# Batch 0, then the weights as fp32, in one SyncE queue, with GpSimd casting from staging buffers; both queries first

## The chip, the cores and the metric

The kernel runs on one core of a Trainium2 chip. The metric is the device time of that core in microseconds; the median of three runs before the change is 317.52 us. The profile is one execution of the same program, recorded by the hardware profiler; its times count from the start of its span. TensorE (PE) multiplies matrices, its weight loads are listed apart as PEld; VectorE (DVE) and ScalarE (ACT) work on tiles, GpSimd (POOL) can cast and issue transfers, and SyncE (SP) only issues transfers.

## What is computed

A linear attention, followed by a gated feed-forward block. Cut to what matters:

```python
q, k, v: (8 batches, 8 heads, 576 positions, 64) float32
q_s = softmax(q, over the 64)             # each row on its own
k_s = softmax(k, over the 576 positions)
kv  = einsum('bhsd,bhse->bhde', k_s, v)   # 64 x 64 for each head
x   = einsum('bhsd,bhde->bhse', q_s, kv)  # then heads side by side: (4608 tokens, 512)

g   = x @ w_gate                          # 512 -> 1536
val = x @ w_val                           # 512 -> 1536
out = (g * sigmoid(g) * val) @ w_out      # 1536 -> 512, float32
```

The kernel leaves out the subtraction of the maximum, which changes nothing in a softmax of small inputs, and multiplies in bf16 with fp32 sums.

## The kernel before

Tokens are handled batch by batch. A batch has 576 tokens and its 8 heads are two groups G of 4 heads; one tile of q, k or v of a group is 128 partitions by 2 by 576 fp32, in rows of 2304 bytes (576 KB in all). The attention of a batch writes its 512 features, transposed, to `xt`, four blocks of 128 feature rows; features are what the feed-forward sums over.

The feed-forward of a token range works in 12 units m of 128 hidden features (`m_unit`, line 286): four matmuls g_ps of `wg`, four u_ps of `wv`, each into PSUM banks, then Silu on ScalarE (`sg`, line 305) and a product on VectorE (`hr`, line 306). For the first 576 tokens every unit has two column parts, 320 and 256. `o_mm` (line 318) then multiplies `hr` with `wo`, 12 matmuls for 128 tokens, and the result is copied out and stored from the SyncE queue.

Everything on each engine is in the order in which the code is written (a manual schedule); the tile pools add the waits for buffers. Pool `ld` has three buffers for each of the tags q, k and v. What stands at the beginning, in order:

- SyncE loads q and k of batch 0, group 0 then group 1 (lines 355 to 357, `load`, line 77).
- GpSimd's queue loads v of batch 0 straight into bf16 tiles `v16`, since that queue can cast on the way (lines 358 to 361); the first of these waits for the first k. Behind them in the same queue come all weights, cast on the way as well: four slices each of `wg` and `wv`, of 256, 384, 384 and 512 columns, taken in turns, then four of `wo` (lines 380 to 383). GpSimd's time goes to issuing them.
- ScalarE takes exponentials of q and k (line 124) in pieces; VectorE sums (line 138) and scales them (line 152); TensorE turns the query (`turn_pe`, line 166), and forms key sums (line 397), kv (`kv_first`, line 411) and x (`x_mm`, line 220). `spin` matmuls on a zero tile fill TensorE's waits.
- SyncE's next loads, batches 1 and 2 (lines 454 and 455), wait for the second wo slice (`w_dma[-3]`).
- The 12 units m of batch 0 follow (line 457), and then attention of batch 1 between four o units (lines 460 to 493), in which ScalarE works in the order: first query, first key, second query, two copies of o results, second key; TensorE turns the first query, forms kv, does an o unit, and turns the second query. `cast_v` (line 127) casts v of later batches on GpSimd.
- Then seven chunks of tokens follow, each with 12 units m, four o units and the attention of a later batch in between.

Of the kernel before, what the change touches and what calls it, by code (L numbers as in the profile page):

```python
# [15 lines left out]
def kernel(  # L16
# [10 lines left out]
    nc = tc.nc  # L27
# [37 lines left out]
    def head_ap(src, b, G, t0=0, t1=T):  # L65
        return bass.AP(
            tensor=src.tensor,
            offset=src[b, 4 * G].offset + 64 * t0,
            ap=[[T * 64, 128], [2 * HSTR, 2], [1, (t1 - t0) * 64]],
        )  # L70

    def load(what, src, b, G, pieces=((0, T),), after=None):
        t_ = ld.tile([128, 2, T * 64], FP32, tag=what, name=what)
        raw[what, b, G] = t_
        last = None
        for t0, t1 in pieces:
            last = nc.sync.dma_start(out=t_[:, :, 64 * t0:64 * t1], in_=head_ap(src, b, G, t0, t1))
            if after is not None:
                tc.add_manual_dep(last.ins, after.ins.name, SYNC, reason="order of loads")
                after = None  # L80
        return last
# [10 lines left out]

    def w_slice(dst, src, c0, n):
        ap = bass.AP(
            tensor=src.tensor,
            offset=src[0, c0].offset,
            ap=[[d_ff, 128], [128 * d_ff, KT], [1, n]],
        )
        return nc.gpsimd.dma_start(out=dst[:, :, c0:c0 + n], in_=ap)

    def wo_slice(m0, n):
        ap = bass.AP(
            tensor=moe_w_out.tensor,
            offset=moe_w_out[m0 * 128, 0].offset,
            ap=[[d_model, 128], [128 * d_model, n], [1, d_model]],
        )
        return nc.gpsimd.dma_start(out=wo[:, m0:m0 + n, :], in_=ap)
# [11 lines left out]
    def exp_of(what, b, G, pieces=((0, T),)):  # L119
        s = st.setdefault((b, G), {})  # L120
        e = s["e" + what] = at.tile([128, T, 2, 64], BF16, tag="e" + what, name="e" + what)
        src = raw[what, b, G].rearrange("p h (t d) -> p t h d", d=64)
        for t0, t1 in pieces:
            nc.scalar.activation(out=e[:, t0:t1], in_=src[:, t0:t1], func=AF.Exp)  # L124
# [7 lines left out]
    def norm_sum(b, G, pieces=((0, T),)):  # L132
        s = st[b, G]
        eq2 = s["eq"].rearrange("p t h d -> p (t h) d")
        rs = at.tile([128, 2 * T], FP32, tag="rs", name="rs")
        first = None
        for t0, t1 in pieces:
            i = nc.vector.reduce_sum(  # L138
                out=rs[:, 2 * t0:2 * t1], in_=eq2[:, 2 * t0:2 * t1, :], axis=mybir.AxisListType.X
            )  # L140
            first = first or i
        rr = s["rr"] = at.tile([128, 2 * T], FP32, tag="rr", name="rr")
        nc.vector.reciprocal(out=rr, in_=rs)
        return first

    def norm_mul(b, G, pieces=((0, T),), engs=None):
        s = st[b, G]
        eq2 = s["eq"].rearrange("p t h d -> p (t h) d")
        qs = s["qs"] = at.tile([128, T, 128], BF16, tag="qs", name="qs")
        for (t0, t1), eng in zip(pieces, engs or (nc.vector, nc.vector)):  # L150
            n = 2 * (t1 - t0)
            eng.tensor_mul(  # L152
                qs[:, t0:t1, :].rearrange("p t (h d) -> p (t h) d", d=64),
                eq2[:, 2 * t0:2 * t1, :],
                s["rr"][:, 2 * t0:2 * t1].to_broadcast([128, n, 64]),
            )
# [129 lines left out]
    def m_unit(c0, n, m, by_part=False):  # L286
# [7 lines left out]
        if by_part:  # L294
            steps.sort(key=lambda a: (a[2], a[0], a[1]))
# [57 lines left out]
    with tc.manual_schedule():  # L353
        kd = []
        for G in range(NG):
            load("q", q, 0, G)
            kd.append(load("k", k, 0, G))
        d = nc.gpsimd.dma_start(out=v16[0], in_=head_ap(v, 0, 0))  # L358
        tc.add_manual_dep(d.ins, kd[0].ins.name, SYNC, reason="order of loads")
        for t0, t1 in BANKS:  # L360
            nc.gpsimd.dma_start(out=v16[1][:, :, 64 * t0:64 * t1], in_=head_ap(v, 0, 1, t0, t1))  # L361
# [11 lines left out]
        exp_of("q", 0, 0, BANKS)  # L373
        exp_of("k", 0, 0)
        exp_of("q", 0, 1, BANKS)
        first = norm_sum(0, 0, BANKS)
        norm_mul(0, 0, BANKS)
        norm_sum(0, 1, BANKS)

        for c0, n in ((0, 256), (256, 384), (640, 384), (1024, 512)):  # L380
            w_slice(wg, moe_w_gate, c0, n)
            w_slice(wv, moe_w_val, c0, n)
        w_dma = [wo_slice(m0, 3) for m0 in (0, 3, 6, 9)]
# [20 lines left out]
        def kv_first(G, t0=0, t1=T):  # L404
            s = st[0, G]
            if t0 == 0:
                s["kv"] = [bank("kv") for _ in range(2)]
            for t in range(t0, t1):
                for g in range(2):
                    r = slice(64 * g, 64 * g + 64)  # L410
                    nc.tensor.matmul(
                        out=s["kv"][g][:, 0:128].rearrange("p (h d) -> p h d", d=64),
                        lhsT=ek_of(0, G, g, t), rhs=v16[G][r, :, 64 * t:64 * t + 64],
                        start=(t == 0), stop=(t == T - 1),
                    )

        def scale_first(G, eng1):
            s = st[0, G]
            kn = s["kn"] = at.tile([128, 2, 128], BF16, tag="kn1", name="kn1")
            nc.scalar.mul(kn[:, 0, :], s["kv"][0][:, 0:128], s["kvr"][:, 0:1])  # L420
            if eng1 is nc.scalar:
                nc.scalar.mul(kn[:, 1, :], s["kv"][1][:, 0:128], s["kvr"][:, 1:2])
            else:
                nc.vector.tensor_scalar_mul(kn[:, 1, :], s["kv"][1][:, 0:128], s["kvr"][:, 1:2])

        spin(8)
        spin(6, first)
        key_sum(0)
        turn_pe(0, 0, 0)
        turn_pe(0, 0, 1)  # L430
        turn_out(0, 0, 0, nc.scalar)
        exp_of("k", 0, 1)
        turn_out(0, 0, 1, nc.scalar)
        norm_mul(0, 1, BANKS)
        spin(6)
        key_sum(1)
        kv_first(0)
        scale_first(0, nc.scalar)
        turn_pe(0, 1, 0)
        turn_pe(0, 1, 1)  # L440
        turn_out(0, 1, 0, nc.vector)
        turn_out(0, 1, 1, nc.vector)
        xp0 = x_mm(0, 0, 0), x_mm(0, 0, 1)
        kv_first(1, *BANKS[0])
        kv_first(1, *BANKS[1])
        x_out(0, 0, 0, xp0[0], (nc.scalar, nc.scalar))
        x_out(0, 0, 1, xp0[1], (nc.vector, None))
        scale_first(1, nc.vector)
        xp1 = x_mm(0, 1, 0), x_mm(0, 1, 1)
        x_out(0, 1, 0, xp1[0], (nc.scalar, nc.vector))  # L450
        x_out(0, 0, 1, xp0[1], (None, nc.vector))
        x_out(0, 1, 1, xp1[1], (nc.scalar, nc.vector))

        load_batch(1, w_dma[-3], by_group=True)
        load_batch(2)

        for m in range(MT):
            m_unit(0, S, m, by_part=(m == 0))
# [124 lines left out]
```

The softmax here doesn't subtract the row's maximum and nothing guards it: scores larger than these inputs give would overflow.

## Time and profile before

| what | value |
|---|---|
| median of three runs | 317.52 us (317.51 to 317.7) |
| the profiled run: time, span | 317.75 us, 316.0 us |
| granted TensorE clock in it | 0.998 of full speed |
| g_ps and u_ps matmuls (line 298) | 110.0 and 109.8 us busy |
| o_ps matmuls (line 322) | 93.0 us busy |
| a GpSimd cast of v, 128x1152 (line 127) | 1146 ns |
| HBM read, written | 37.75 MB, 9.44 MB |

How to read it: busy time is summed over the span, and matmuls overlap one another and their weight loads, so the shares add to more than the span. The page cuts the span into 40 slices of 7.9 us and gives the busy tenths of each engine in each. A timeline row is start, duration, engine, line, operation, output from input, and in brackets how long the engine had been idle and what ended that. A chain row is start, duration and what the end of the run can be followed back to. A window row is the stretch, its length, the busy time of PE, PEld, DVE, ACT and POOL with their instructions, then TensorE's clock, the share of the 16 DMA engines in use (over 1 where packets overlap) and GB/s. For a queue that casts, the bytes are those written.

### The profile page before, as it was taken

Reading aid. Unit: us, or ns where it says so; the run is one execution under the profiler, and the core shown is the slowest. Engines: PE = TensorE matmul, PEld = TensorE weight load, DVE = VectorE, ACT = ScalarE, POOL = GpSimd, SP = SyncE. Lnnn points to the kernel's source line nnn. Section 1 sums busy time; section 2 is a strip of 40 time slices with the busy share of each in tenths; the row PEclk is TensorE's granted clock in tenths of the full one; section 3 lists DMA queues with packets and bytes.
Section 4 is the critical chain, followed back from the end, with each engine's and each line's share of the span. In section 5 each row is a group of like instructions: output and inputs, shape, how many; then the busy total and the mean of one; then the engine's idle time right before and its main releaser. Section 6 shows DMA issues by size and latency. Waiting matters only on the chain.

```text
span 316.0 us, 4856 instructions
## 1 busy us (share of the span) xinstructions
PE 304.7 (96%) x1865; PEld 152.0 (48%) x1894; DVE 163.2 (52%) x277; ACT 147.6 (47%) x218; POOL 28.0 (9%) x35
## 2 busy tenths in 40 slices
PE   6799999999999999999999999999999999999994
PEld 2477744554444444544454444544454444444443
DVE  3834476685754566455835492639354333423421
ACT  4743488634663465447354637355743113312300
POOL 2930021100200020002000200020000000000000
PEclk9999999999999999999999999999999999999999
DMA  7999999269246806490629253944310202020124
GB/s 269 183 204 207 296 393 391 68 160 364 50 91 179 338 17 128 112 394 11 141 68 352 97 110 66 322 162 103 66 41 0 65 3 66 0 68 3 31 68 102
DMA packets 39304, 45.75 MB, mean 145 GB/s; under 512 B 16368, under 2 KB 23024, under 8 KB 39280
## 3 DMA queue, kind: packets, MB, share of 16 engines
q1 hardware_dynamic: 32480, 39.99, 42.0%
q0 software_dynamic: 6640, 5.31, 10.9%
q8 instruction: 15, 0.25, 0.3%
q10 hardware_dynamic: 160, 0.13, 0.2%
q14 instruction: 9, 0.07, 0.1%
HBM read 37.75 MB, written 9.44 MB: 149 GB/s over the span
## 4 chain that ended last, share of the span: by engine, by line
PE 88%; DMA 4%; DVE 3%; ACT 2%; issue 1%; POOL 1%; SPq 0%; DVEq 0%
PE g_ps L298 29%; PE u_ps L298 29%; PE o_ps L322 25%; PE kv L191 3%; DMA wv<-in_moe_w_val_dram 2%; DMA k<-in_k_dram 2%; DVE rs L138 1%; PE xp L267 1%; DVE qs L152 1%; PE o_ps L342 1%; ACT L124 1%; ACT eq L124 1%; POOL v L361 0%; PE tp L166 0%; POOL v L358 0%
## 5 line engine op out<-in xcount | busy, mean ns | idle before, releaser
L305 ACT ACTIVATE sg<-g_ps 128x512 bf16<-128x512 f32 (+2 forms) x120 | 65.1, 554 | 139.1 <-PE g_ps L298 120.7
L306 DVE TENSOR_TENSOR hr<-sg,u_ps 128x512 bf16<-128x512 bf16 (+2 forms) x120 | 74.5, 630 | 87.8 <-PE u_ps L298 80.4
L298 PE MATMUL g_ps<-xt,wg 128*128 128x512 bf16 (+2 forms) x469 | 110.0, 358 | 1.0 <-ACT xt L111 0.2
L298 PE MATMUL u_ps<-xt,wv 128*128 128x512 bf16 (+2 forms) x468 | 109.8, 357 | 1.2 <-DMA wv<-in_moe_w_val_dram 0.5
L322 PE MATMUL o_ps<-wo,hr 128*128 128x512 bf16 x414 | 93.0, 379 | 0.4 <-issue 0.2
L298 PEld LDWEIGHTS <-wv 128*128 128x128 bf16 x480 | 46.9, 98 | 47.2 <-DMA wv<-in_moe_w_val_dram 0.9
L298 PEld LDWEIGHTS <-wg 128*128 128x128 bf16 x480 | 45.8, 98 | 45.3 <-issue 0.7
L322 PEld LDWEIGHTS <-hr 128*128 128x128 bf16 x420 | 40.9, 98 | 49.1
L113 DVE COPY o_sb<-o_ps 128x512 f32<-128x512 f32 x33 | 22.4, 680 | 39.2 <-PE o_ps L322 37.3
L127 POOL CAST vb<-v 128x1152 bf16<-128x1152 f32 x14 | 16.0, 1146 | 174.3 <-DMA v<-in_v_dram 111.8
L138 DVE TENSOR_REDUCE rs<-eq 128x18 f32<-128x1152 bf16 (+2 forms) x18 | 21.7, 1214 | 13.2 <-ACT eq L124 13.2
L152 DVE TENSOR_TENSOR qs<-eq,rr 128x1152 bf16<-128x1152 bf16 (+2 forms) x18 | 22.1, 1237 | 0.1
L124 ACT ACTIVATE eq<-q 128x1152 bf16<-128x1152 f32 (+2 forms) x18 | 18.1, 1050 | 4.5 <-DMA q<-in_q_dram 4.4
L124 ACT ACTIVATE ek<-k 128x1152 bf16<-128x1152 f32 x16 | 18.0, 1158 | 0.3 <-DMA k<-in_k_dram 0.2
L305 ACT ACT_TABLE_LOAD x12 | 15.4, 1283 | 0.2
L124 ACT ACT_TABLE_LOAD x11 | 14.1, 1283 | 0.2
L388 PE MATMUL idle<-zero 128*128 128x512 bf16 x20 | 6.1, 459 | 3.0 <-DVE rs L138 1.8
L191 PE MATMUL kv<-vb,ek 64*128 64x129 bf16 x252 | 8.7, 217 | 0.0
L191 PEld LDWEIGHTS <-ek 64*128 64x128 bf16 x252 | 7.3, 94 | 2.7 <-ACT sg L305 2.1
L275 ACT CAST xt<-xp 128x512 bf16<-128x512 f32 x12 | 6.4, 588 | 3.6 <-PE xp L267 3.6
L276 DVE CAST xt<-xp 128x512 bf16<-128x512 f32 x12 | 7.7, 683 | 0.0
L347 ACT COPY o_sb<-o_ps 128x128 f32<-128x128 f32 x2 | 0.5, 265 | 13.3 <-DVE o_sb L346 13.3
(46 smaller groups left out, 70.2 us busy)
## 6 DMA issues: line engine op xcount, KB each, us to landing
q<-in_q_dram SPq DMA_DIRECT2D x16, 576.0 KB, 5.6
k<-in_k_dram SPq DMA_DIRECT2D x16, 576.0 KB, 7.3
out_dram<-o_sb SPq DMA_DIRECT2D x70, 128.0 KB, 2.3
v<-in_v_dram SPq DMA_DIRECT2D x14, 576.0 KB, 9.0
wo<-in_moe_w_out_dram POOLq DMA_DIRECT2D x4, 384.0 KB, 16.3
wg<-in_moe_w_gate_dram POOLq DMA_DIRECT2D x2, 384.0 KB, 9.7
wv<-in_moe_w_val_dram POOLq DMA_DIRECT2D x2, 384.0 KB, 10.7
wg<-in_moe_w_gate_dram POOLq DMA_DIRECT2D x1, 512.0 KB, 13.7
```

The costliest lines, as they stand in the source:

```text
L113: eng.tensor_copy(out=out, in_=in_)
L124: nc.scalar.activation(out=e[:, t0:t1], in_=src[:, t0:t1], func=AF.Exp)
L127: nc.gpsimd.tensor_copy(out=vbs[G][:, :, 0:128].rearrange("p t (h d) -> p t h d", d=64), in_=raw["v", b, G].rearrange("p h (t d) -> p t h ...
L138: i = nc.vector.reduce_sum(out=rs[:, 2 * t0:2 * t1], in_=eq2[:, 2 * t0:2 * t1, :], axis=mybir.AxisListType.X)
L152: eng.tensor_mul(qs[:, t0:t1, :].rearrange("p t (h d) -> p (t h) d", d=64), eq2[:, 2 * t0:2 * t1, :], s["rr"][:, 2 * t0:2 * t1].to_broadca ...
L191: nc.tensor.matmul(out=kv[g][:, c:c + 129], lhsT=ek_of(b, G, g, t), rhs=vbs[G][r, t, 0:129], start=(t == 0), stop=(t == T - 1),)
L275: nc.scalar.copy(out=xt[:, 2 * G, c0:c0 + 512], in_=main[G][0])
L276: nc.vector.tensor_copy(out=xt[:, 2 * G + 1, c0:c0 + 512], in_=main[G][1])
L298: nc.tensor.matmul(out=gu[a][i][:, 0:w_], lhsT=(wg, wv)[a][:, kk, ms], rhs=xt[:, kk, c:c + w_], start=(kk == 0), stop=(kk == KT - 1),)
L305: nc.scalar.activation(out=sg[:, 0:w_], in_=g_ps[:, 0:w_], func=AF.Silu)
L306: nc.vector.tensor_mul(hr[:, m, r:r + w_], sg[:, 0:w_], u_ps[:, 0:w_])
L322: nc.tensor.matmul(out=o_ps, lhsT=hr[:, m, r0:r0 + 128], rhs=wo[:, m, :], start=(m == 0), stop=(m == MT - 1),)
```

## The change

1. GpSimd issues no transfers. The queue of SyncE carries, in this order: both queries of batch 0, the first key, the first v, the second key, the second v; then all weights as fp32; then batches 1 and 2. The queries, the second key and the second v are each loaded as two halves of one row of heads (`by_head`), and the exponentials and sums of these are taken in the same halves.
2. The weights land in the buffers of the pool `ld`, tags q, k and v in turn (`w_load`), 20 transfers: `wg` and `wv` in slices of 128, 128 and then 256 columns, `wo` in six slices of two. GpSimd casts each to bf16 (`staged`), after v of batch 0.
3. The last half of v is cast by VectorE (384 columns) and ScalarE (192) (`cast_last`).
4. The order at the beginning is another one: both turns of queries before kv of group 0, the second kv in halves by head, other counts of `spin`, other engines for some copies.
5. Batch 1's loads no longer name a weight transfer to wait for; and `by_part`, which did the first unit m part by part, is gone.

```diff
-        t_ = ld.tile([128, 2, T * 64], FP32, tag=what, name=what)
-        for t0, t1 in pieces:
-            last = nc.sync.dma_start(out=t_[:, :, 64 * t0:64 * t1], in_=head_ap(src, b, G, t0, t1))
+        for h in ((0, 1), (1, 2)) if by_head else ((0, 2),):
+            last = nc.sync.dma_start(out=t_[:, h[0]:h[1], :], in_=head_ap(src, b, G, h))
...
+    staged = []
+
+    def w_load(dst, ap):
+        tag = ("q", "k", "v")[len(staged) % 3]
+        t_ = ld.tile([128, 2, T * 64], FP32, tag=tag, name="w" + tag)
+        n0, n1 = dst.shape[1:]
+        view = t_.rearrange("p h c -> p (h c)")[:, 0:n0 * n1].rearrange("p (a b) -> p a b", b=n1)
+        staged.append((dst, view))
+        nc.sync.dma_start(out=view, in_=ap)
...
-        for G in range(NG):
-            load("q", q, 0, G)
-            kd.append(load("k", k, 0, G))
-        d = nc.gpsimd.dma_start(out=v16[0], in_=head_ap(v, 0, 0))
-        tc.add_manual_dep(d.ins, kd[0].ins.name, SYNC, reason="order of loads")
-        for t0, t1 in BANKS:
-            nc.gpsimd.dma_start(out=v16[1][:, :, 64 * t0:64 * t1], in_=head_ap(v, 0, 1, t0, t1))
+        load("q", q, 0, 0, by_head=True)
+        load("q", q, 0, 1, by_head=True)
+        load("k", k, 0, 0)
+        load("v", v, 0, 0)
+        load("k", k, 0, 1, by_head=True)
+        load("v", v, 0, 1, by_head=True)
+        for c0, n in [(0, 128), (128, 128)] + [(c, 256) for c in range(256, d_ff, 256)]:
+            w_slice(wg, moe_w_gate, c0, n)
+            w_slice(wv, moe_w_val, c0, n)
+        for m0 in range(0, MT, 2):
+            wo_slice(m0, 2)
...
-        for c0, n in ((0, 256), (256, 384), (640, 384), (1024, 512)):
-            w_slice(wg, moe_w_gate, c0, n)
-            w_slice(wv, moe_w_val, c0, n)
-        w_dma = [wo_slice(m0, 3) for m0 in (0, 3, 6, 9)]
+        nc.gpsimd.tensor_copy(out=v16[0], in_=raw["v", 0, 0])
+        nc.gpsimd.tensor_copy(out=v16[1][:, 0, :], in_=raw["v", 0, 1][:, 0, :])
+        for dst, src in staged:
+            nc.gpsimd.tensor_copy(out=dst, in_=src)
...
+        def cast_last():
+            n = 64 * 6
+            nc.vector.tensor_copy(out=v16[1][:, 1, 0:n], in_=raw["v", 0, 1][:, 1, 0:n])
+            nc.scalar.copy(out=v16[1][:, 1, n:], in_=raw["v", 0, 1][:, 1, n:])
...
+        spin(12)
+        spin(4, first)
+        turn_pe(0, 0, 0)
+        turn_out(0, 0, 0, nc.scalar)
+        turn_pe(0, 0, 1)
+        turn_out(0, 0, 1, nc.scalar)
+        spin(7)
+        exp_of("k", 0, 0)
+        norm_mul(0, 1, BANKS)
+        key_sum(0)
+        turn_pe(0, 1, 0)
+        exp_of("k", 0, 1, True)
+        turn_out(0, 1, 0, nc.vector)
+        turn_pe(0, 1, 1)
+        turn_out(0, 1, 1, nc.vector)
+        kv_first(0)
+        scale_first(0)
+        key_sum(1)
+        cast_last()
+        xp0 = x_mm(0, 0, 0), x_mm(0, 0, 1)
+        kv_first(1, 0, 1)
+        x_out(0, 0, 0, xp0[0])
+        kv_first(1, 1, 2)
+        scale_first(1)
+        x_out(0, 0, 1, xp0[1])
+        x_one(0, 1)
 
-        load_batch(1, w_dma[-3], by_group=True)
+        load_batch(1, by_group=True)
         load_batch(2)
```

## The prediction

> **What bounds the kernel now.** I read the page's first three parts, then the chain of waits for the first 20 us, then ScalarE's and VectorE's order of work at 36 to 50 us, then windows. The page's totals:
>
> ```profile
> span 316.0 us, 4856 instructions
> PE 304.7 (96%) x1865; PEld 152.0 (48%) x1894; DVE 163.2 (52%) x277; ACT 147.6 (47%) x218; POOL 28.0 (9%) x35
> DMA  7999999269246806490629253944310202020124
> GB/s 269 183 204 207 296 393 391 68 160 364 50 91 179 338 17 128 112 394 11 141 68 352 97 110 66 322 162 103 66 41 0 65 3 66 0 68 3 31 68 102
> q1 hardware_dynamic: 32480, 39.99, 42.0%
> q0 software_dynamic: 6640, 5.31, 10.9%
> ```
>
> TensorE is busy 96% of the span, so only its idle time, some 11 us, can be won or added to; 4.6 of it lie in the first 15 us (the windows of that stretch sum to 10.4 us busy). A slice is 7.9 us: in the first seven (55 us) the DMA row reads 7, then 9s. The transfers of batches 0 to 2 and of all weights are one unbroken backlog. The GB/s row sags in slices 1 to 3 because the casting queue q0 is counted in written bf16: its 5.31 MB are 10.62 MB of fp32 read, 200 to 207 GB/s are some 410 read.
>
> The chain shows when steady work starts:
>
> ```profile
> 9.38 6.77 DMA wv<-in_moe_w_val_dram
> 16.15 0.05 issue
> 16.20 0.72 PE u_ps L298 x4
> 16.92 0.44 PE g_ps L298 x4
> ```
>
> The first wv slice ends the wait, at 16.20. Four matmuls of g_ps (0.44 us) had been done before, so TensorE runs as if from 15.76 and is then all but gapless to 44.5. The next place where an arrival matters is batch 1 (ScalarE first, then VectorE, then weight loads):
>
> ```profile
> 39.03 1.28 ACT L124 ACT_TABLE_LOAD   x1
> 40.32 1.16 ACT L124 ACTIVATE eq<-q 128x1152 bf16<-128x1152 f32 x1
> 41.39 1.15 ACT L124 ACTIVATE ek<-k 128x1152 bf16<-128x1152 f32 x1
> 43.63 1.16 ACT L124 ACTIVATE eq<-q 128x1152 bf16<-128x1152 f32 x1 [1.09 <-DMA q<-in_q_dram]
> ...
> 44.83 1.35 DVE L138 TENSOR_REDUCE rs<-eq 128x18 f32<-128x1152 bf16 x1 [0.26 <-ACT eq L124]
> ...
> 47.27 1.76 DVE L152 TENSOR_TENSOR qs<-eq,rr 128x1152 bf16<-128x1152 bf16 x1
> ...
> 44.62 0.50 PEld L166 LDWEIGHTS <-qs 128*128 128x128 bf16 x9 [0.58 <-DVE qs L152]
> 49.08 0.51 PEld L166 LDWEIGHTS <-qs 128*128 128x128 bf16 x9 [0.38 <-DVE qs L152]
> ```
>
> The exponential of batch 1's second query starts at 43.63, when its load lands (idle 1.09 us before it). From there VectorE works without a pause (reduce, reciprocal, two scales, product) until 49.03, and the second turn starts at 49.08, just as TensorE runs out (its xp matmuls before it end at 48.99). So this load has no slack: a microsecond later there is a microsecond on the end. The first query has some: the table load, not the DMA, sets 40.32.
>
> [...] from 8 to 55 us the DMA row is full whichever queue runs, so going over to one queue frees no bandwidth. [...] the product at 47.27, beside a GpSimd cast (46.67 to 47.82), took 1.76 us, the one at 43.21 alone 1.36.
>
> **The change part by part.**
>
> *SyncE's row cost.* Two windows:
>
> ```profile
> 25.00:30.00 5.00, 5.00 (x43) 3.99 (x41) 2.09 (x6) 1.71 (x6) 0.00 (x0) 1.00 1.24 206
> 40.00:45.00 5.00, 4.91 (x28) 2.24 (x27) 3.32 (x5) 3.90 (x5) 1.14 (x1) 1.00 1.05 392
> ```
>
> At 40 to 45 only 2304-byte rows flow: 392 GB/s, 24.5 per engine, 94 ns a row, and 1.50 us for a load of 589,824 B. [...] A 1 KiB row [...] I take 45. A 2 KiB row: [...] I take 83. A 512 B row: [...] I take 26. All three are estimates.
>
> *Weights on SyncE.* Per engine: four 128-column slices, 128 x 4 / 16 = 32 rows each, 128 x 26 ns = 3.3 us; ten 256-column slices, 320 rows x 45 = 14.4; six wo slices, 96 rows x 83 = 8.0. Sum 25.7 us (24.4 to 26.7). Through the casting queue the same 9.44 MB take 9.44/0.41 = 23.0 us at its steady 206 (412 read), more in its first slices. So GpSimd's transfers were the faster ones.
>
> *Batch 0.* The six loads come first. The third landed at 8.17 before (exp of the second query); three more at 1.50 end at 12.7. SyncE's ten issues at 0.47 us are all out by 6 us, off the path.
>
> *Arrival of batch 1.* 12.7 + 25.7 = 38.4 for the last weight; batch 1 follows in the same queue, its fourth load is the second query: 38.4 + 4 x 1.50 = 44.4. Before: 43.63. Difference +0.8 (−0.5 to +1.8 from the row prices). The first query lands at 39.9, within its slack.
>
> *GpSimd casts.* 1152 columns took 1146 ns, so a 1024-column slice takes about 1.02, a 512-column one 0.51: 4 x 0.51 + 16 x 1.02 = 18.4 us beside 25.7 of transfers. Each is done before the next slice lands (1.4 us apart). A unit m takes TensorE 1.96 us and uses up 1024 columns, 1.02 us of casting. The last wo cast ends at 39.6; its rows are read last in the first o_ps, about 41. Cost nothing, hidden under g_ps and u_ps. The trace has no cast of these shapes (4x256); were one twice as slow, see the rivals.
>
> *Reused buffers.* Every tag has three buffers, so transfer i waits for the cast of slice i − 9. Nine slices are 4 MB, 10 us of backlog: SyncE never runs dry. Behind a waiting issue stand only later loads. Batch 1's loads no longer wait for w_dma[-3], but for casts some 10 us older.
>
> *Head order.* The last v half lands at 12.7. Then half casts on VectorE and ScalarE (0.4, from the 128x320 casts' 0.35 to 0.4), 18 kv matmuls (0.65; 0.75 before for wider ones), the scale (0.37), xp (0.45), the first xt cast (0.4): 15.0. Before it was 15.76. Handovers can add 0.5, so TensorE starts 0.3 to 0.8 earlier; I take 0.6. The wv slice needed by then lands at 12.7 + 1.7 and is cast by 14.9. But TensorE meets the same turn at about 49.9, so what it wins here it waits there. by_head exponentials and sums split the same elements differently, with 2 pieces before and after; by_part's removal reorders 16 matmuls. Both nothing: they lie ahead of that wait.
>
> *Sum.* 316.0 + 0.8 = 316.8 of span. The profiled run took 317.75 for its 316.0, the median run 317.52; 317.52 + 0.8 = 318.3.
>
> **Rivals.** About 0.2%, 0.64 us, is what I call no change.
> 1. *The likeliest: batch 1 arrives later* by 0.3 to 1.8: 317.8 to 319.4, at 318.3. For: backlog unbroken to 55 us, no slack at 49.08. Against: the price of a 1 KiB row is not in the trace. 0.50.
> 2. *TensorE leads.* [...] the load comes 0.6 or more early and the head's gain reaches the end: 316.9 at 0.6 won, 316.5 at 1.0. For: the wait at 16.20 goes away. Against: at 206 the old queue already read 412 GB/s. 0.20.
> 3. *A wash:* arrival within 0.3 of before: 317.5. 0.20.
> 4. *The staging ring starves the loads.* If a strided cast takes 2 us instead of 1.02, sixteen take 32 us from about 17 on; the last ends at 49, and o_ps, which needs it at 41, waits up to 8 us: 322 to 326; at 1.5 us it is 24 us, done at 41, and costs nothing to 1 us. It decides from about 1.5 us a cast on. For: one GpSimd queue casts all. Against: a cast with a 9x128 pattern ran at 1 ns a column. 0.10.
> That the change doesn't do what it says is ruled out by the built order: no transfer is left on GpSimd.
>
> **How the numbers follow.** Slower by over 0.2%: 0.40 of the first case's 0.50 (its part above 318.16) and the fourth's 0.10, 0.50. No change: 0.10 and the wash, 0.30. Faster: 0.20. The range goes from 316.5, the head's gain at its best, to 320.2, the first case with a slow start of TensorE added; what starves badly is left out. The first case alone is 317.8 to 319.4.
>
> **What would show it.** Right: q0 gone; 360 to 380 GB/s over 17 to 31 us; u_ps in step from about 15; ScalarE idle before the second batch 1 query, which starts near 44.4; a gap of TensorE ahead of the turn near 50. Wrong: that query at or before 43.2; or g_ps or o_ps waiting for GpSimd between 16 and 42; or POOL casts of 1024 columns well over 1.1 us.

## The result, and the profile after

The changed kernel takes 321.39 us, the median of four runs (320.99 to 321.78), against 317.51 us for the kernel before beside it (317.26 to 317.70): a ratio of 1.0123, with a 95% interval of 1.0105 to 1.0140. It is slower by 3.9 us. The forecast had the sign but not the size: it said 318.3, with 320.2 at the outer edge. The profiled run took 321.72 us with a span of 319.9, 3.9 more than before. Most lines of code have moved down by 3 to 8, so that the exponential is now line 132, the turn 171, g_ps and u_ps 301.

From the page of the kernel after, the rows that answer those shown of before, and two more:

```profile
span 319.9 us, 4979 instructions
POOL 0466651200200020002000200020000000000000
PEclk9779999999999999999999999999999999999999
DMA  7999999539263917292439443853320202020124
GB/s 258 349 348 355 387 391 391 172 65 345 108 139 78 369 64 130 65 356 102 102 70 320 158 100 74 260 219 71 73 64 0 50 18 66 2 66 1 33 69 98
q1 hardware_dynamic: 42112, 50.60, 52.1%
```

The casting queue is gone and SyncE's queue has 9,632 more packets. The GB/s row shows fp32 at 348 to 355 in slices 1 to 3, where before some 410 were read through the casting queue. The DMA row is full for 55 us as before, so the same transfers ahead of batch 1 take longer. In slices 1 and 2 TensorE's granted clock is down to 7 tenths; before it was at 9 tenths or more in every slice.

The chain of waits of the kernel after (start, duration, what) left the transfers only with the second query of batch 1; before, it had left them at 16.15:

```profile
17.10 9.17 DMA wq<-in_moe_w_val_dram
26.27 9.35 DMA wq<-in_moe_w_out_dram
35.67 1.05 POOL wo L387
36.74 10.27 DMA q<-in_q_dram
47.03 1.17 ACT eq L132
```

The chain passes through a cast on GpSimd, because the second query lands in a buffer that a slice of `wo` had used. That cast does not set the time: the transfer is issued 10.27 us before it lands, and the four loads of batch 1 follow the last slice of `wo` at the full pace of the queue, in 5.96 us. So the queue never ran dry.

The timeline of the kernel after at that place (start, duration, engine, line, operation, and in brackets the idle time before it and what ended it), ScalarE first, then VectorE, then TensorE:

```profile
40.96 1.28 ACT L132 ACT_TABLE_LOAD   x1
42.58 1.16 ACT L132 ACTIVATE eq<-q 128x1152 bf16<-128x1152 f32 x1 [0.33 <-DMA q<-in_q_dram]
44.02 1.16 ACT L132 ACTIVATE ek<-k 128x1152 bf16<-128x1152 f32 x1 [0.28 <-DMA k<-in_k_dram]
47.03 1.17 ACT L132 ACTIVATE eq<-q 128x1152 bf16<-128x1152 f32 x1 [1.86 <-DMA q<-in_q_dram]
...
48.23 1.35 DVE L145 TENSOR_REDUCE rs<-eq 128x18 f32<-128x1152 bf16 x1 [1.42 <-ACT eq L132]
50.67 2.05 DVE L157 TENSOR_TENSOR qs<-eq,rr 128x1152 bf16<-128x1152 bf16 x1
...
46.87 0.68 PE L171 MATMUL tp<-ident,qs 128*128 128x128 bf16 x9 [0.41 <-DVE qs L157]
52.78 0.68 PE L171 MATMUL tp<-ident,qs 128*128 128x128 bf16 x9 [1.13 <-DVE qs L157]
```

The second query is exponentiated at 47.03 instead of 43.63 (+3.40), the second turn starts at 52.78 instead of 49.08 (+3.70), and TensorE stood idle 1.13 us for it. The first query, too, is now waited for (0.33 us on ScalarE, and TensorE stands idle 0.41 at the first turn), which it was not before. From there to the end nothing differs much: the span less the start of the second turn is 267.12 us here and 266.92 before. In all fifteen profiles of this study it is between 266.8 and 267.2. So the start of the second turn tells the whole time, and the question is what sets it. Two things come together there: TensorE, which must have done batch 0 (its progress can be read from ScalarE's table load, the change from Silu to the exponential, which follows the last Silu of batch 0 and stands at 39.03 before and 40.96 after), and the arrival of the second query, to which the exponential, VectorE's work and the turn are chained.

TensorE's own lag comes from the head, the work on batch 0 ahead of the first unit m. Its first units in the kernel after, in the timeline, come first below; windows of the same kernel follow (stretch, length, busy PE, PEld, DVE, ACT, POOL, clock, DMA share, GB/s):

```profile
15.73 2.10 PE L301 MATMUL g_ps<-xt,wg 128*128 128x320 bf16 x8
17.63 2.09 PE L301 MATMUL u_ps<-xt,wv 128*128 128x320 bf16 x8
19.55 1.16 PE L301 MATMUL g_ps<-xt,wg 128*128 128x320 bf16 x8
```

The second unit m of the kernel before, and then the windows of the kernel after:

```profile
17.63 1.15 PE L298 MATMUL g_ps<-xt,wg 128*128 128x320 bf16 x8
```

```profile
12.00:13.00 1.00, 0.87 (x29) 0.68 (x26) 0.46 (x2) 0.66 (x2) 0.58 (x1) 0.87 1.15 309
13.00:14.00 1.00, 1.00 (x28) 0.56 (x27) 0.76 (x2) 0.68 (x2) 0.09 (x1) 0.50 1.18 292
19.00:20.00 1.00, 1.00 (x8) 0.66 (x7) 0.35 (x1) 0.00 (x0) 0.31 (x1) 0.72 1.09 344
```

Eight matmuls of 320 columns take 2.1 us instead of 1.15. Between these windows the clock was 0.50 throughout; the means of 0.87 and 0.72 put its fall to one half at about 12.74 and its return at about 19.56, 6.8 us later (an estimate from these windows). The second unit starts at 19.55, and at 17.63 before.

### The profile page after: what moved, and what is told of

It is laid out like the page before. It is cut to its first block, busy times and chain, and to the rows that moved or that the text cites. A ratio compares the mean times of both kernels' runs of the same rounds, so it can differ in the third digit from the quotient of the medians.

```text
span 319.9 us, 4979 instructions
## 1 busy us (share of the span) xinstructions
PE 310.6 (97%) x1915; PEld 154.0 (48%) x1915; DVE 164.1 (51%) x279; ACT 148.2 (46%) x219; POOL 39.3 (12%) x42
## 4 chain that ended last, share of the span: by engine, by line
PE 82%; DMA 13%; DVE 1%; SPq 1%; ACT 1%; POOL 0%; issue 0%
PE o_ps L325 26%; PE g_ps L301 26%; PE u_ps L301 26%; DMA wq<-in_moe_w_val_dram 5%; DMA q<-in_q_dram 3%; DMA wq<-in_moe_w_out_dram 3%; PE kv L196 2%; DMA v<-in_v_dram 2%; PE xp L272 1%; PE o_ps L345 1%; SPq L77 1%; DVE qs L157 1%; DVE rs L145 0%; ACT eq L132 0%; POOL wo L387 0%
## 5 line engine op out<-in xcount | busy, mean ns | idle before, releaser
L301 PE MATMUL g_ps<-xt,wg 128*128 128x512 bf16 (+2 forms) x480 | 112.3, 361 | 0.2 <-ACT xt L119 0.2
L301 PE MATMUL u_ps<-xt,wv 128*128 128x512 bf16 (+2 forms) x480 | 111.9, 360 | 0.0
L135 POOL CAST vb<-v 128x1152 bf16<-128x1152 f32 x14 | 17.2, 1229 | 156.3 <-DMA v<-in_v_dram 155.4
L145 DVE TENSOR_REDUCE rs<-eq 128x18 f32<-128x1152 bf16 (+1 forms) x18 | 21.7, 1215 | 13.3 <-ACT eq L132 13.3
L132 ACT ACTIVATE eq<-q 128x1152 bf16<-128x1152 f32 (+1 forms) x18 | 18.4, 1052 | 4.7 <-DMA q<-in_q_dram 4.5
L132 ACT ACTIVATE ek<-k 128x1152 bf16<-128x1152 f32 (+1 forms) x17 | 18.2, 1104 | 1.5 <-DMA k<-in_k_dram 1.4
L392 PE MATMUL idle<-zero 128*128 128x512 bf16 x23 | 7.6, 499 | 1.2 <-DVE sel L373 1.2
```

The costliest lines, as they stand in the source:

```text
L132: nc.scalar.activation(out=e[:, :, h], in_=src[:, :, h], func=AF.Exp)
L135: nc.gpsimd.tensor_copy(out=vbs[G][:, :, 0:128].rearrange("p t (h d) -> p t h d", d=64), in_=raw["v", b, G].rearrange("p h (t d) -> p t h ...
L145: i = nc.vector.reduce_sum(out=rs[:, :, h], in_=s["eq"][:, :, h, :], axis=mybir.AxisListType.X)
L301: nc.tensor.matmul(out=gu[a][i][:, 0:w_], lhsT=(wg, wv)[a][:, kk, ms], rhs=xt[:, kk, c:c + w_], start=(kk == 0), stop=(kk == KT - 1),)
L392: i = nc.tensor.matmul(out=idle, lhsT=zero[:, 0:128], rhs=zero, start=True, stop=True)
```

## The experiments

Theory A: the end is set by the later of two lags which run side by side, the arrival of batch 1 (+3.4 us) and TensorE's late start (+1.9); in the kernel after it is the arrival. Rival B: the late start, with the halved clock in it, sets the end. Others are named in the expectations: C, that GpSimd's casts set it, and D to F and R on single points.

### 1. Holding the clock up

```diff
         turn_out(0, 1, 1, nc.vector)
+        spin(3)
         kv_first(0)
...
+        spin(2)
         cast_last()
...
+        spin(2)
         kv_first(1, 1, 2)
         scale_first(1)
+        spin(3)
```

> The changed kernel with ten more spin matmuls on the zero tile in the head (3 before kv_first(0), 2 before the first xp, 2 before the second half of the second kv, 3 before the second xp), so that TensorE's clock is not halved from 12.9 to 19.7 us. Theory A (the arrival of batch 1's second query, 47.0 us, sets the end): TensorE's units start some 1.9 us earlier and it waits that much longer near 45 to 53; time 321.4, within 0.4. Rival B (the halved clock and late start of the units set the end): 319.5, 1.9 less. Rival C (GpSimd's casts set it): no change, 321.4.

Measured: 321.80 us, ratio 1.0138 (1.0113 to 1.0162). The clock stayed at 1.0 (0.999 to 1.000 in the four executions; an execution of the kernel after has 1.000 without the spins, so it is not shown that they held it) and the table load came at 40.18, 0.78 earlier than in the kernel after; the second query was exponentiated at 46.70 and TensorE idled more, 0.83, 0.32 and 1.05 us at the first turn, kv and the second turn. What TensorE won at the head it waited for at batch 1. B falls as what sets the end here. The four runs of the kernel after say the same: one with a clock of 1.000 took 321.78, one with 0.989 took 321.72.

### 2. A shorter backlog ahead of batch 1

Three of the six wo transfers are left out; their rows take the data of the others, so that the casts remain (and these rows of `w_out` are not the true ones). The tags of the buffers go on in turn.

```diff
...
-        for m0 in range(0, MT, 2):
+        for m0 in range(0, MT, 4):
             wo_slice(m0, 2)
+            staged.append((wo[:, m0 + 2:m0 + 4, :], staged[-1][1]))
```

> The changed kernel with three of the six wo transfers left out (their casts stay, and take the slice before; so half of w_out is wrong and the output is not the reference's). The backlog ahead of batch 1 is 4.05 us shorter (3 x 1.35). Theory A: second query of batch 1 exponentiated at 43.0 instead of 47.0; the end moves until TensorE's late start shows (1.9 late against the kernel before): 319.4, between 319.0 and 320.0. Rival B: 321.4. Rival C (20 casts as before): 321.4.

Measured: 320.18 us (1.0084, 1.0061 to 1.0107), 1.2 us less than the kernel after. The timeline of this run:

```profile
41.33 1.28 ACT L132 ACT_TABLE_LOAD   x1
44.74 1.15 ACT L132 ACTIVATE eq<-q 128x1152 bf16<-128x1152 f32 x1
51.23 0.68 PE L171 MATMUL tp<-ident,qs 128*128 128x128 bf16 x9
```

No bracket stands on any of the three: the second query is there before ScalarE wants it, and TensorE goes into the second turn without a wait. The arrival no longer counts, and the other lag comes to light: the table load is 2.30 later than before (the clock was halved in this run too, 0.50 over 15 to 20 us), the second turn 2.15. C falls with it, since the casts are as many as in the kernel after and the run is 1.2 us shorter. The time lay 0.2 above A's range, because TensorE's start was later still than in the kernel after.

### 3. Both lags at once

The edits of 1 and 2 together; the same three wo transfers are left out.

> Both edits: three wo transfers left out and ten more spins (half of w_out is wrong again). Theory A: both lags are gone, 317.5, between 316.6 and 318.0. Rival B: as with the spins alone, 319.5. Rival C: 321.4.

Measured: 319.02 us (1.0051, 1.0034 to 1.0068), 1.5 us above what A said. In the profile the table load came at 39.97, 0.94 late though the clock stood at 1.0, and the second turn at 49.87, 0.79 late, without a wait. So the rest was TensorE's start again: the last v of batch 0 landed at 13.76 (13.18 in the kernel after), and ten spins lay on the path. Whether that was all of it, 5 and 6 had to tell.

### 4. Whole loads for batch 0

```diff
-        for h in ((0, 1), (1, 2)) if by_head else ((0, 2),):
+        for h in ((0, 2),):
```

> The changed kernel with the six loads of batch 0 whole (576 KB each) instead of in halves; exponentials and sums stay split. In the runs with halves the DMA moved 287 to 354 GB/s at 2.5 to 5 us, in the kernel before 387. Theory F (the halves cost the early transfers 0.5 to 1 us, which the whole backlog inherits): last v of batch 0 at 12.6 to 12.9 instead of 13.2 to 14.0, second query of batch 1 at 46.3 instead of 47.0, time 320.8. Rival: the halves cost nothing, v at 13.2 or later, 321.4.

Measured: 320.57 us (1.0095, 1.0081 to 1.0108). The clock stayed at 1.0 here by itself. Its timeline, TensorE's first units, then the place of batch 1:

```profile
15.83 1.26 PE L301 MATMUL g_ps<-xt,wg 128*128 128x320 bf16 x8
16.92 1.14 PE L301 MATMUL u_ps<-xt,wv 128*128 128x320 bf16 x8
17.90 1.14 PE L301 MATMUL g_ps<-xt,wg 128*128 128x320 bf16 x8
...
39.30 1.28 ACT L132 ACT_TABLE_LOAD   x1
46.04 1.16 ACT L132 ACTIVATE eq<-q 128x1152 bf16<-128x1152 f32 x1 [1.85 <-DMA q<-in_q_dram]
45.84 0.68 PE L171 MATMUL tp<-ident,qs 128*128 128x128 bf16 x9 [1.04 <-DVE qs L157]
51.61 0.68 PE L171 MATMUL tp<-ident,qs 128*128 128x128 bf16 x9 [0.96 <-DVE qs L157]
```

This is the plainest evidence for A. TensorE is only 0.27 us behind the kernel before at the table load, and yet the kernel is 3.0 us slower: it waits 1.04 us at the first turn, 0.33 at kv and 0.96 at the second turn, each for work that hangs on batch 1's loads.

The time agreed with the number put down for the halves, but these two profiles alone do not bear out the reason given for it. The first slice of 1,024 columns is cast at 18.12 here and at 18.27 in the kernel after, so whole loads won 0.15 us between them. The other 0.84 us of the 0.99 by which the second query comes earlier lie further back in the queue, in two slow steps of the kernel after that this profile does not have in that size (see the point on delays below). The other profiles speak for the halves' cost: the last v landed at 13.18 to 14.02 in the five with halved loads and the weights in the same queue (the kernel after, 1, 2, 3 and 7), and at 12.72 to 13.06 in the four with whole loads (4, 5, 6 and 8); the first slice of 1,024 columns was cast at 18.27 to 18.98 against 17.80 to 18.16. Whole loads are some 0.6 us earlier on average, and the kernel after was the best of the halved ones. How much of the 0.8 us between the medians is owed to them is open.

### 5. Spins, whole loads and the short backlog

The edits of 1, 2 and 4 together; three wo transfers are left out.

> The run with three wo transfers left out and ten more spins (319.0), with whole loads of batch 0 as well (half of w_out is wrong, as there). Theory F: TensorE, which sets the end there, starts its units 0.6 to 0.9 us earlier, 318.1 to 318.4. Rival (the order of the head, not the halves, makes the start late): 319.0.

Measured: 319.75 us (1.0078, 1.0059 to 1.0097), worse than run 3 and 1.4 above what was expected. Nothing waits for the second query (44.47), but the table load stands at 41.05. Against the run of 4, kv of group 0 starts at 13.42 instead of 12.77, and the last xp of batch 0 (the matmuls that form x) at 17.19 instead of 15.44: with whole loads the turns of the queries come later (the second group's at 11.84, in run 3 at 10.35), and each spin then stands in front of work that run 4 does at once.

### 6. The short backlog with whole loads, no spins

> The kernel after with whole loads of batch 0 and with three of the six wo transfers left out (their rows take the other transfers' data, so the output's values differ); no spins added. Theory A (two lags side by side, the longer decides: the arrival of batch 1 and TensorE's start): the start is that of the run with whole loads (units at 15.8, table load 39.3, 0.3 after before), and the second query of batch 1, which landed at 46.0 there, is freed of 3 x 1.35 = 4.05 us, so that no load is waited for at 43 to 50; both lags then are 0.3 or less and the time is 317.8 (317.4 to 318.3); 318.3 to 318.9 if the clock halves in the head. Rival R (fp32 weights staged through GpSimd cost something besides, which the 319.0 and 319.75 of the two runs with spins and a short backlog showed, and which I put down to the spins): 319.0 to 319.8 though both lags are gone.

Three wo transfers are left out here too. Measured: 318.95 us over ten runs (1.0054, 1.0032 to 1.0076), 1.15 above A's number and just under the rival's. The single runs say more than the median. Two had a mean clock of 0.986 and took 321.17 and 321.08; the other eight, at 0.995 to 1.000, took 318.16 to 319.12. The lower clock, which costs the kernel after nothing (321.72 us at 0.989, 321.78 at 1.000), goes with some 2.3 us more here, where no arrival hides it. That is what two lags side by side would do. The profiled run (318.48 us, clock 0.998, span 0.6 above before):

```profile
20.15 1.04 POOL L388 CAST wv<-wv 128x1024 bf16<-128x1024 f32 x1 [1.30 <-DMA wv<-in_moe_w_val_dram]
21.24 1.16 PE L301 MATMUL u_ps<-xt,wv 128*128 128x320 bf16 x8 [0.57 <-POOL wv L388]
39.71 1.28 ACT L132 ACT_TABLE_LOAD   x1
43.13 1.15 ACT L132 ACTIVATE eq<-q 128x1152 bf16<-128x1152 f32 x1
49.62 0.68 PE L171 MATMUL tp<-ident,qs 128*128 128x128 bf16 x9
```

Its second unit started at 17.57, no later than before (17.63). What it lost, it lost at 21.24: a wv slice was cast 2.35 us after the one ahead of it instead of 1.50, and TensorE waited for that cast. The second turn is 0.54 late and the span 0.6. So in this execution the two lags explain the time and no further cost of staging is seen. Of the other seven runs with a high clock there is no profile; six of them took 0.15 to 0.64 us more than the profiled one, which may be such late slices, but that was not shown.

### 7. Longer rows for the weights

The wg and wv slices from column 512 on become two row blocks by 512 columns, so that a row in memory is 2 KB instead of 1 KB; the bytes are the same.

```diff
-        for c0, n in [(0, 128), (128, 128)] + [(c, 256) for c in range(256, d_ff, 256)]:
+        for c0, n in [(0, 128), (128, 128), (256, 256)]:
...
+        for c0 in (512, 1024):
+            for dst, src in ((wg, moe_w_gate), (wv, moe_w_val)):
+                for kk in (0, 2):
+                    w_load(dst[:, kk:kk + 2, c0:c0 + 512], bass.AP(
...
+                        ap=[[d_ff, 128], [128 * d_ff, 2], [1, 512]],
...
```

> The changed kernel with wg and wv from column 512 on loaded as 2 row blocks by 512 columns (rows of 2 KB) instead of 4 by 256 (rows of 1 KB): eight transfers at some 1.35 us instead of 1.50, the same bytes. Theory A (row length sets the price, arrival sets the end): second query of batch 1 at 45.8 instead of 47.0, time 320.2 to 320.8. Rival D (the transfers are slow for another reason, such as the engines taking turns or GpSimd's buffers): second query at 47.0, 321.4.

Measured: 320.72 us (1.0099, 1.0085 to 1.0113). GpSimd's timeline shows the step between slices, first the kernel after, then this one:

```profile
27.85 1.04 POOL L387 CAST wg<-wk 128x1024 bf16<-128x1024 f32 x1 [0.47 <-DMA wk<-in_moe_w_gate_dram]
29.36 1.04 POOL L387 CAST wv<-wv 128x1024 bf16<-128x1024 f32 x1 [0.46 <-DMA wv<-in_moe_w_val_dram]
30.84 1.04 POOL L387 CAST wg<-wq 128x1024 bf16<-128x1024 f32 x1 [0.44 <-DMA wq<-in_moe_w_gate_dram]
32.95 1.04 POOL L387 CAST wv<-wk 128x1024 bf16<-128x1024 f32 x1 [1.06 <-DMA wk<-in_moe_w_val_dram]
```

```profile
23.33 1.04 POOL L395 CAST wg<-wk 128x1024 bf16<-128x1024 f32 x1 [0.31 <-DMA wk<-in_moe_w_gate_dram]
24.68 1.04 POOL L395 CAST wv<-wv 128x1024 bf16<-128x1024 f32 x1 [0.30 <-DMA wv<-in_moe_w_val_dram]
26.03 1.04 POOL L395 CAST wv<-wq 128x1024 bf16<-128x1024 f32 x1 [0.31 <-DMA wq<-in_moe_w_val_dram]
```

Steps of 1.50 us (and one of 2.11) become steps of 1.35. The same 512 KB in 16 rows per engine instead of 32 take 0.15 us less: about 9.4 ns for each row saved. So the length of the rows does count, and D, that the transfers are slow for another reason, falls for these steps. The second query came at 45.51, 1.5 us earlier, but TensorE's lag took over (table load 41.19), with the clock partly halved (0.76 over 12.9 to 20 us) and two waits for slices, 0.46 and 0.69 us: the second turn, at 51.22, shows no wait.

### 8. Longer rows, whole loads and spins

The edits of 1, 4 and 7 together.

> The changed kernel with three things mended: whole loads of batch 0, ten more spins, and 2 KB rows from column 512 on. Theory A: second query of batch 1 at about 45.0 (47.0 less 0.5 less 1.5), and TensorE's start at full clock near 15.9 with a stall of 1 to 2 us at unit 4, whose four slices land by 26; both lags 1.4 to 2, so 319.0 to 320.0, still slower than the kernel before because the fp32 transfers fill the queue some 1.4 us longer. Rival: if the clock or the halves were all of it, 317.5.

Measured: 319.99 us (1.0074, 1.0058 to 1.0089), at the edge of what was expected. The second query came at 45.05; the table load, behind the spins, at 41.10; the second turn at 51.00 without a wait. Again the one lag uncovers the other.

### 9 and 10. Either part alone

In 9 the kernel after keeps its head and its loads of batch 0, but the weights go through GpSimd's casting queue, as in the kernel before:

```diff
...
         nc.gpsimd.tensor_copy(out=v16[0], in_=raw["v", 0, 0])
+        w_slice(wg, moe_w_gate, 0, 256)
+        w_slice(wv, moe_w_val, 0, 256)
         nc.gpsimd.tensor_copy(out=v16[1][:, 0, :], in_=raw["v", 0, 1][:, 0, :])
-        for dst, src in staged:
-            nc.gpsimd.tensor_copy(out=dst, in_=src)
...
```

> The changed kernel's head, but the weights through GpSimd's casting queue again in the slices of the kernel before (wg and wv of 256, 384, 384, 512 columns, wo in four), issued after the cast of the first v, and batch 1 waits for the second wo slice again. No staging casts. Theory A: the casting queue reads the same 9.44 MB in some 24 us instead of 27.9, so the second query of batch 1 is at 43 to 44.5: 317.5 to 319.5, the upper end if TensorE's clock is halved in the head here too. Rival B: 321 if the clock is halved, 319.5 if not. Rival C: 317.5, as nothing is cast on GpSimd.

Measured: 320.26 us (1.0094, 1.0064 to 1.0125), above A's range. The second query came at 45.35 and the second turn, at TensorE's pace, at 51.21; the table load stood at 41.18, with the clock partly halved (0.76 over 12.9 to 20 us). With 209 GB/s written at 25 to 30 us, 418 read, the queue was as fast as before; but GpSimd issues its first slice only behind its cast of the first v, at 11.85 instead of 8.63.

In 10 the kernel before gets only the staged weights (`w_load` with the same slices and casts, and batch 1 without its wait); its head and the loads of batch 0 stay, v through the casting queue.

```diff
...
-        for c0, n in ((0, 256), (256, 384), (640, 384), (1024, 512)):
+        for c0, n in [(0, 128), (128, 128)] + [(c, 256) for c in range(256, d_ff, 256)]:
...
-        w_dma = [wo_slice(m0, 3) for m0 in (0, 3, 6, 9)]
+        for m0 in range(0, MT, 2):
+            wo_slice(m0, 2)
+        for dst, src in staged:
+            nc.gpsimd.tensor_copy(out=dst, in_=src)
...
-        load_batch(1, w_dma[-3], by_group=True)
+        load_batch(1, by_group=True)
```

> The kernel before with the weights part of the change alone: all weights as fp32 in SyncE's queue behind q and k of batch 0, in the changed kernel's slices, cast by GpSimd from the shared staging buffers; v of batch 0 stays in GpSimd's queue and the head's order stays. Theory A (two lags side by side, the longer one counts): this alone brings the late arrival, second query of batch 1 at 46.5 to 47.5, 320.8 to 321.8. Rival E (the parts add up: 2.75 of the 3.9 come from the head, as the run with the casting queue would have it): 318.7.

Measured: 320.96 us (1.0121, 1.0099 to 1.0143), nearly the whole loss, with none of the new head. The timeline of this run:

```profile
13.68 0.68 PE L422 MATMUL kv<-v,ek 64*128 64x128 bf16 x18 [1.44 <-DMA v<-in_v_dram]
...
46.75 1.16 ACT L132 ACTIVATE eq<-q 128x1152 bf16<-128x1152 f32 x1 [1.81 <-DMA q<-in_q_dram]
47.67 0.68 PE L174 MATMUL tp<-ident,qs 128*128 128x128 bf16 x9 [0.75 <-DVE qs L160]
51.61 0.44 PE L228 MATMUL xp<-qt,kn 64*64 64x320 bf16 x8
52.19 0.68 PE L174 MATMUL tp<-ident,qs 128*128 128x128 bf16 x9
```

The staged weights alone bring the second query 3.12 us late. And v, which comes in the other queue, lands later as well: kv starts at 13.68 instead of 11.43 and waits 1.44 us for it, and 0.77 for the second group. So TensorE is late here as well: its table load comes 2.39 late, and it waits 0.75 us at the first turn for a product that ran beside a cast of v (2.01 us instead of 1.36). From there to the second turn it has no gap. Both lags end together, the query's product at 52.13 and TensorE's own work at 52.05, so this run shows the late arrival, but not that the arrival alone would have cost 3.4. Parts of 3.4 and 2.8 us do not add to 3.9, as they would if they lay one behind the other.

### 11. What a late second query costs the kernel before

The kernel before, with the order of batch 1's loads changed: the second query is fifth instead of fourth, one load of 1.50 us later.

```diff
-            order = [(w, s, G) for G in range(NG) for w, s in qkv]
+            src = dict(qkv)
+            order = [(w, src[w], G) for w, G in (("q", 0), ("k", 0), ("v", 0), ("k", 1), ("q", 1), ("v", 1))]
```

> The kernel before with batch 1 loaded in the order q, k, v, k, q, v instead of q, k, v, q, k, v, nothing else. The second query lands one load (1.46 us) later. Theory A (no slack there): 318.9, between 318.6 and 319.2. If there is slack at that load: 317.5.

Measured: 318.38 us (1.0042, 1.0025 to 1.0058): +0.8, not the +1.4 expected, and not nothing, as the rival with slack had it. The timeline of this run:

```profile
44.60 1.16 ACT L125 ACTIVATE eq<-q 128x1152 bf16<-128x1152 f32 x1 [2.36 <-DMA q<-in_q_dram]
46.15 1.15 POOL L128 CAST vb<-v 128x1152 bf16<-128x1152 f32 x1 [3.37 <-DMA v<-in_v_dram]
48.24 1.35 DVE L153 TENSOR_TENSOR qs<-eq,rr 128x1152 bf16<-128x1152 bf16 x1
49.64 0.68 PE L167 MATMUL tp<-ident,qs 128*128 128x128 bf16 x9 [0.43 <-DVE qs L153]
```

The query came 0.97 late, the turn 0.56: the product took 1.35 us instead of 1.76, since it now starts at 48.24, when the cast of v on GpSimd (46.15 to 47.30) is over; in the kernel before it ran beside that cast. That there is no slack was right; that a microsecond there is a microsecond at the end was not quite.

### 12 and 13. Relieving the kernel before

If both lags are tight, the kernel before should gain from an earlier second query only together with an earlier start. In 12 the query is loaded third and the first weight slices are 128, 256, 512 and 640 columns; in 13, whose edit is shown, they are 128, 256, 384, 384 and 384.

```diff
-            order = [(w, s, G) for G in range(NG) for w, s in qkv]
+            src = dict(qkv)
+            order = [(w, src[w], G) for w, G in (("q", 0), ("k", 0), ("q", 1), ("v", 0), ("k", 1), ("v", 1))]
...
-        for c0, n in ((0, 256), (256, 384), (640, 384), (1024, 512)):
+        for c0, n in ((0, 128), (128, 256), (384, 384), (768, 384), (1152, 384)):
```

> The kernel before with batch 1 loaded in the order q, k, q, v, k, v, and the weights' slices of 128, 256, 512 and 640 columns instead of 256, 384, 384 and 512, so that the first unit's weights land earlier. Theory A: the second query lands 1.46 us earlier and no longer holds TensorE, whose start moves from 15.76 to 15.3 at best: 317.0 to 317.3. If x of batch 0 or the first value's cast holds TensorE instead: 317.5.

> The kernel before with the weights' slices 128, 256, 384, 384, 384 columns and batch 1 in the order q, k, q, v, k, v. In the run with slices of 128, 256, 512, 640 TensorE started 0.44 us earlier but waited 1.33 us at unit 3 for the slice of 512. Theory A: without that wait the 0.44 reaches the end, 317.1. If unit 3 or a later one waits again: 317.5 or more.

Measured: 318.99 us (1.0046, 1.0033 to 1.0058) and 318.11 us (1.0014, 1.0006 to 1.0021). Both miss. One line of the timeline of each, 12 and then 13:

```profile
23.57 1.15 PE L299 MATMUL u_ps<-xt,wv 128*128 128x320 bf16 x8 [1.33 <-DMA wv<-in_moe_w_val_dram]
```

```profile
18.76 1.15 PE L299 MATMUL u_ps<-xt,wv 128*128 128x320 bf16 x8 [0.89 <-DMA wv<-in_moe_w_val_dram]
```

The second query was there in time, but the smaller first slices let TensorE come to its second unit 0.45 or 0.90 us earlier, only to wait 1.33 or 0.89 us for the next wv slice. No kernel of the study was faster than the kernel before.

### The runs together

Times in us within each profiled span. "Not waited for": the query had landed before ScalarE came to it.

| kernel | table load | second query | second turn | span |
|---|---|---|---|---|
| before | 39.03 | 43.63 | 49.08 | 316.0 |
| after | 40.96 | 47.03 | 52.78 | 319.9 |
| 1, spins | 40.18 | 46.70 | 52.37 | 319.4 |
| 4, whole loads | 39.30 | 46.04 | 51.61 | 318.5 |
| 10, weights alone | 41.42 | 46.75 | 52.19 | 319.2 |
| 11, late query | 38.73 | 44.60 | 49.64 | 316.6 |
| 2, short backlog | 41.33 | not waited for | 51.23 | 318.2 |
| 6, short, whole loads | 39.71 | not waited for | 49.62 | 316.6 |
| 5, short, whole, spins | 41.05 | not waited for | 50.94 | 317.9 |

In the lower three rows the second turn comes 9.9 us after the table load, which is TensorE's own pace. In the upper six it comes 5.0 to 5.8 us after the second query, by how long the product takes beside a cast. The later of the two decides; in the kernel before and in run 10 they fall together. Of the six runs left out of the table, 3, 7, 8 and 9 go at TensorE's pace (9.9 to 10.0 us); 12 and 13 come 10.4 and 10.3 us after the table load, since TensorE waits 0.61 us at the first turn and 0.32 at kv there.

## Why the prediction was right and wrong

Right: where it happens and how. The arrival of batch 1 sets the end, SyncE's backlog is what delays it, and a gain at the head would have been waited for at the second turn. (The first query was said to be within its slack; it was not, by 0.33 us.) Right, too, that staging does not starve: casts of 1,024 columns take 1.04 us (1.02 said) and each waits for its transfer, so rival 4 is out. The measured numbers stand against the steps as follows.

*Arrival, the term that failed.* It said 44.4; the profile has 47.03, 2.63 us more. By stretches:

| stretch | said | measured | more |
|---|---|---|---|
| last v of batch 0 landed | 12.7 | 13.18 | 0.5 |
| four slices of 128 columns | 3.3 | 3.62 | 0.3 |
| ten slices of 256 columns | 14.4 | 16.15 | 1.75 |
| six of wo | 8.0 | 8.12 | 0.1 |
| four loads of batch 1 | 6.0 | 5.96 | 0 |

So the mechanism held, and what was mis-sized is the time of the transfers ahead of batch 1: 12.7 us for batch 0 and 25.7 for the weights were said, 13.18 and 27.89 were measured. Two errors make it up. The first is the price of a row. The trace of the kernel before has it for one length alone, 94 ns for 2,304 B; the 26, 45 and 83 ns for the shorter rows, and the ranges that go with them, were the author's estimates and are shown by no trace of that kernel. Measured in the backlog of the kernel after are 1.50 us for 32 rows of 1 KB, 47 ns each; 0.9 us for 32 rows of 512 B, 28 ns; 1.35 us for 16 rows of 2 KB, 84 ns. The four lengths lie on one line: the 47 and the 94 ns make 0.0367 ns for a byte and 9.4 ns for a row besides (an estimate from these two), which gives 28.2 for 512 B and 84.6 for 2 KB. At the measured prices the weights take 26.7 us (an estimate from 128 rows of 28 ns, 320 of 47 and 96 of 84), the upper end of the prediction's own range, and that explains 1.0 of the 2.63. In the window 25 to 30 us it shows as 348 GB/s where the prediction looked for 360 to 380.

The second is what had no term at all. The last v landed 0.5 late: loads of 1.50 us were the price of a running queue of whole loads, and in the window of 2.5 to 5.0 us the kernel after, with halves, moves 346 GB/s where run 4, with whole loads, moves 395. (Run 4's last v still landed at 13.02, so the halves do not explain all of it.) And 1.15 us lie in two steps, 18.27 to 20.32 and 30.84 to 32.95, of 2.05 and 2.11 us instead of 1.50. Where such steps fall, and how long they are, differs from one execution to the next: in the profile of run 1 the same steps have about 0.1 us at most beyond 1.50; run 4 has one of 0.4, run 6 one of 0.85, run 3 one of 1.55, in other places each time. But of the ten profiles with staged weights only that of run 1 has less than some 0.4 us of them in all, so a term of that kind belongs in the sum. An instruction fetch of 16 KB on its own queue stands ahead of both steps of the kernel after (at 16.7 and 30.1 us); that it makes them was not shown, so the cause stays open. How much of the profile's +3.4 is this execution's own can't be told apart exactly: run 1, with 0.1 us of such delay but a last v at 14.02, has +3.1, and run 4, with 0.4 us, has +2.4.

*No slack at the second query.* Right (runs 4 and 11), with a correction of up to 0.7 us for the product, which takes 1.35 us alone and 1.75 to 2.09 where a GpSimd cast of v began 0.27 to 0.60 us before it (nine products in eight profiles). From the query's +3.40 to the turn's +3.70 the product adds 0.3, and 0.2 more comes in after the turn: 3.9.

*The head.* It said TensorE starts 0.6 us earlier. The first g_ps came at 15.73, about when TensorE ran as if from before (15.76 by the prediction; 15.67 by its second unit at 17.63 and 1.96 a unit), and not at 15.2: the last v was 0.5 late, and from 12.74 the clock was halved, which no step had considered. The kv matmuls of the second group, 36 of 64 columns, took 1.14 us at the halved clock and 0.70 at the full clock of run 4. What makes the clock fall is not shown: from 8 to 12 us TensorE was busy for 2.97 of the 4 us in the kernel after, and for 2.96 in run 1 and 2.71 in run 4, which both kept their clock. The error cost nothing here, since the arrival lay over it; run 6 shows what it costs without. Rival 2, TensorE leading with a gain from the head, falls: even at the full clock (run 4) the second unit started 0.27 later than before.

*The size, then.* The first case's mechanism, read at the top of the author's own price range (+1.8 instead of +0.8), with 0.5 for batch 0, some 0.1 to 1.1 for delays, and 0.5 for the product and the rest: +2.9 to +3.9. The four runs lie from 3.5 to 4.3 above the 317.51 of the kernel before, so up to 0.4 of the slower ones is not accounted for.

## What to carry to other kernels

When a change lengthens a backlog that other work waits for, count rows as well as bytes, and take the price of a row from a full queue, at the length that is planned or at two others: the 94 ns of a 2,304 B row, shared out by bytes, would make 41.8 for 1 KB (an estimate), and 47 were measured. Look for the place where two chains meet, and note for each by how much it leads: here the removal of either lag alone uncovered the other, and parts measured alone (3.4 and 2.8 us) did not add to the whole (3.9). A transfer that casts on its way may be worth its engine's time: 418 GB/s were read through it (run 9), 348 through the plain queue in rows of 1 KB and 386 in rows of 2 KB (run 7).

## What was not expected of the hardware

- The clock of TensorE fell to one half for 6.8 us in the head of the kernel after, in some executions and not in others of the same kernel (mean clock 0.989 and 1.000). In run 6 the executions with a mean clock of 0.986 took 321.1 to 321.2 us, those with 0.995 or more 318.2 to 319.1.
- In a full queue a row cost 28 ns at 512 B, 47 at 1 KB, 84 at 2 KB and 94 at 2,304 B: about 9 ns for a row besides a price by bytes (an estimate from these four).
- Single steps of a steady backlog are 0.1 to 1.55 us longer, in places that differ from one execution to the next; the cause is open.
- Spins are not free: run 5, with ten of them and a clock of 0.991 to 1.000, took 1.0 us more by the median than the eight executions of run 6 with a clock of 0.995 or more.
